# Retention and a feed-forward layer on one core: block 0's stores go ahead of the transposing transfers, and four other steps change places

## The chip, the core and the metric

The kernel runs on one core of a Trainium2 chip. The core has a matrix engine (TensorE, in the rows PE, its weight loads PEld), VectorE (DVE), ScalarE (ACT), GpSimd (POOL) and SyncE (SP). Only PE multiplies matrices; it writes to PSUM, eight banks of 128 partitions by 2 KB. DVE and ACT read PSUM, POOL reads and writes only SBUF, the working memory. Transfers between memory and SBUF are issued here by SP (nearly all), by POOL (the weights) and by ACT (a few), and 16 DMA engines carry them out. The metric is the device time of one execution in microseconds, the median of several runs.

## The reference

For every batch b of 4 and head h of 8, over 768 positions t, with 64 values per head:

```
state = gamma[h] * state + outer(k[t], v[t])      # 64 x 64
y[t]  = (1/8) * q[t] @ state
```

Then x is y with the heads side by side, 3072 tokens of 512 values, and

```
hid = x @ w_in                                    # 512 -> 2048
g   = max(hid, 0) + alpha * min(hid, 0)           # alpha per hidden column
out = g @ w_out                                   # 2048 -> 512, float32
```

## The kernel before

**Tiles and blocks.** The 3072 tokens are cut into twelve units of 256 tokens (a unit is u in the code, three to a batch; the change's short name calls them tiles), and two units make a block n, of six. Retention is done by chunks of 128 tokens (c = 0, 1 of a unit), with a running 64 x 64 state for each head.

**Retention of a unit.** `load` (line 132) brings k, q and v. `rescale` (L152) multiplies k and q by powers of gamma into the fp16 tile kdq; `cast_v` (L166 on ACT, L168 on POOL) makes vx, v in fp16. kq, which holds k and q with the head's values along the partitions, comes from kdq either by PE (`turn_pe`, L182, units 0 to 3) or by a transposing transfer on SP's queue (`turn_dma`, L172, units 4 to 11). `sum_mm` (L215) forms a chunk's sum of outer products; `state` adds it to the running state on DVE (L239, tile ss), multiplies by the decay (L240 on POOL, tile tf; at a batch's first chunk L236 on DVE does that alone) and copies it to fp16 tiles tg (L251 on ACT, L253 on POOL). `score_mm` (L265, tiles sca and scb) forms k q products, `masks` (L277, tiles m) applies the causal mask on DVE, and `out_mm` (L294 with tg, L309 with m) gives y, which ACT copies into xT (L327).

**Feed-forward of a block.** `ffn1(n)` is 64 matmuls of 512 columns (L374) in sixteen turns of four: a turn fills one PSUM bank hps, ACT takes from it hm = relu(-hps) (L385, three buffers), and DVE makes gt (L387) from both. In block 1 the first eight of the sixteen hidden column groups are split by unit: eight turns of eight matmuls with 256 columns, then eight of four with 512. Block 0's second product is `ffn2`, 64 matmuls in four tiles of 128 tokens (ops, L410); ACT copies each tile into os (L419), SP stores it (L423). os has three buffers, so the fourth copy waits for the first store to land.

Blocks 1 to 5 use `ffn2_seven`: the product of 2 x 2 quarters in seven quarter products instead of eight, each of 16 matmuls of 256 columns (L453, banks ox, oy, oz). It needs sums of quarters: of the weights once (`w_sums`, L345, tile wsum) and of the tokens in each block (`g_sums`, L358, tile gs, four sums i = 0 to 3 over eight column groups, which can be cut by lo and hi). Between products ACT keeps a partial result (L468, tile cu) and DVE adds another to it (L473).

**What sets the order.** The order is written by hand: each engine carries out its instructions in the order of the program, and waits where an operand or a buffer isn't ready. `ffn1`, `ffn2` and `ffn2_seven` are generators; `tick(gen, m)` lets one go on by m matmuls, and the retention steps of the next block stand between the ticks. A quarter product takes 16 ticks. `gen` is `ffn2(0)` ahead of the loop and `half` is `ffn1(1)`. `behind(i, gate)` makes POOL's rescaling wait for a DVE sum.

Of the kernel before, what the change touches and what calls it, by code (L numbers as in the profile page):

```python
# [21 lines left out]
def kernel(  # L22
# [13 lines left out]
    NFT = d_ff // 128  # L36
# [45 lines left out]
    HF, HM = NFT // 2, d_model // 2  # L82
    wsum = sbp.tile([128, 4, HF, HM], F16, tag="wsum", name="wsum")

    def ps(bank, name, dt=FP, n=512):
        return psp.tile([128, n], dt, tag=f"b{bank}", name=name)
# [34 lines left out]
    def load(u, parts="kqv"):  # L121
        b, c = divmod(u, UPB)
        t = staged.setdefault(u, {})
        for nm in parts:
            src = {"k": k, "q": q, "v": v}[nm[0]]
            if nm[0] not in t:
                t[nm[0]] = sbp.tile(
                    [128, H, 2 * D], FP, tag=f"{nm[0]}s", bufs=3, name=f"{nm[0]}s{u}"
                )
            h = slice(0, H) if len(nm) == 1 else slice(4 * int(nm[1]), 4 * int(nm[1]) + 4)  # L130
            hold(
                nc.sync.dma_start(  # L132
                    out=t[nm[0]][:, h, :],
                    in_=src[b, h, U * c : U * c + U, :].rearrange(
                        "h (p r) d -> p h (r d)", r=2
                    ),
                )
            )
# [23 lines left out]
    def cast_v(eng, u, h0=0, h1=H):  # L162
        o = unit(u)[2][:, h0:h1].rearrange("p h r d -> p (h r d)")
        i = staged[u]["v"][:, h0:h1].rearrange("p h x -> p (h x)")
        if eng is nc.scalar:
            eng.activation(out=o, in_=i, func=COPY, bias=0.0, scale=1.0)  # L166
        else:
            eng.tensor_copy(out=o, in_=i)  # L168

    def turn_dma(u):  # L170
        kdq, kq, _ = unit(u)
        nc.sync.dma_start_transpose(out=kq, in_=kdq.rearrange("p t r h d -> p (t r h d)"))  # L172
# [54 lines left out]
    def state(u, c, eng, copy="gg"):  # L227

        if (u, c) in sums:
            state_copy(state_sum(u, c, eng), copy)  # L230
# [43 lines left out]
    def masks(u, hh, parts=(0, 1)):  # L274
        for a in parts:
            m2 = sbp.tile([128, 2, 2, 128], F16, tag=f"m2{a}{hh}", bufs=2, name=f"m2{a}{hh}")
            nc.vector.tensor_tensor(  # L277
                out=m2,
                in0=live[u, hh][a].rearrange("p (r a i) -> p r a i", r=2, a=2),
                in1=mask.unsqueeze(2).to_broadcast([128, 2, 2, 128]),  # L280
                op=MULT,
            )
            live[u, hh][a] = m2
# [53 lines left out]
    def w_sums(i, lo, hi):  # L337

        w = w_out_all.rearrange("p (k f) (j e) -> p k f j e", k=2, j=2)
        w12, w21, w22 = w[:, 0, lo:hi, 1, :], w[:, 1, lo:hi, 0, :], w[:, 1, lo:hi, 1, :]  # L340
        t1, t2, t3, t4 = (wsum[:, x, lo:hi, :] for x in range(4))
        o, a, b = (
            (t1, w12, w[:, 0, lo:hi, 0, :]), (t2, w22, t1), (t3, w22, w12), (t4, w21, t2)
        )[i]
        return nc.vector.tensor_tensor(out=o, in0=a, in1=b, op=SUB)  # L345

    def g_sums(n, i, lo, hi):

        if n not in gsums:
            gsums[n] = sbp.tile([128, 4, HF, U], F16, tag="gt", bufs=2, name=f"gs{n}")  # L350
        g = gts[n].rearrange("p (k f) (j t) -> p k f j t", k=2, j=2)
        a11, a12 = g[:, 0, lo:hi, 0, :], g[:, 1, lo:hi, 0, :]
        a21, a22 = g[:, 0, lo:hi, 1, :], g[:, 1, lo:hi, 1, :]
        s1, s2, s3, s4 = (gsums[n][:, x, lo:hi, :] for x in range(4))
        o, a, b, op = (
            (s1, a21, a22, ADD), (s2, s1, a11, SUB), (s3, a11, a21, SUB), (s4, a12, s2, SUB)
        )[i]
        return nc.vector.tensor_tensor(out=o, in0=a, in1=b, op=op)  # L358

    def ffn1(n, banks, apart=0):  # L360


        gt = sbp.tile([128, NFT, TB], F16, tag="gt", bufs=2, name=f"gt{n}")
        gts[n] = gt
        turns = [(f, 2, ul, ul + 1) for ul in range(2) for f in range(0, apart, 2)]
        rest = range(apart, NFT)
        if apart == 0:
            rest = [f + x for f in range(HF) for x in (0, HF)]
        turns += [(f, 1, 0, 2) for f in rest]
        for i, (f0, nf, lo, hi) in enumerate(turns):  # L370
            hps = ps(banks[i % len(banks)], "hps").rearrange("p (f t) -> p f t", f=nf)
            for f in range(nf):
                for hp in range(4):
                    nc.tensor.matmul(  # L374
                        out=hps[:, f, :].rearrange("p (u t) -> p u t", t=U),
                        lhsT=w_in_all[:, hp, 128 * (f0 + f) : 128 * (f0 + f) + 128],
                        rhs=xT[n][:, lo:hi, hp, :],
                        start=(hp == 0),
                        stop=(hp == 3),
                    )  # L380
                    if f < nf - 1 or hp < 3:
                        yield
            hm = sbp.tile([128, TB], FP, tag="hm", bufs=3, name="hm")
            hm = hm.rearrange("p (f t) -> p f t", f=nf)
            nc.scalar.activation(out=hm, in_=hps, func=RELU, bias=0.0, scale=-1.0)  # L385
            for f in range(nf):
                nc.vector.scalar_tensor_tensor(  # L387
                    out=gt[:, f0 + f, U * lo : U * hi],
                    in0=hm[:, f, :],
                    scalar=oma_sb[:, f0 + f : f0 + f + 1],  # L390
                    in1=hps[:, f, :],
                    op0=MULT,
                    op1=ADD,
                )
            if n > 0 and f0 in (HF + 5, NFT - 1):
                lo, hi = (0, 6) if f0 < NFT - 1 else (6, HF)
                g_sums(n, 0, lo, hi)
                g_sums(n, 1, lo, hi)
            yield
# [136 lines left out]
    def tick(gen, m=10**6):  # L536
        for _ in range(m):
            if next(gen, 1) == 1:
                return
# [13 lines left out]
    V, G, A = nc.vector, nc.gpsimd, nc.scalar  # L553
# [84 lines left out]
    get_wo(2)  # L638
    out_mm(1, (4, 5))
    gen = ffn1(0, (2, 3, 6, 7, 0, 1, 2, 3, 6, 7, 4, 5, 0, 1, 2, 3), apart=4)  # L640
    tick(gen)


    gen = ffn2(0, (0, 1, 2, 3), parts=4)
    half = ffn1(1, (6, 7, 4, 5, 4, 5, 0, 1, 2, 3, 0, 1, 4, 5, 6, 7), apart=8)
    turn_pe(2, 0, 5)
    tick(gen, 5)
# [12 lines left out]
    rescale(G, 3, 0, 4, 8)  # L660
    rescale(G, 3, 1, 4, 8)
    cast_v(G, 3)
    tick(gen, 9)
    out_mm(2, (4, 5))
    tick(gen, 10)
# [6 lines left out]
    masks(3, 0)  # L672
    sum_mm(3, (6, 7))
    state(3, 0, G, "ga")
    w_sums(0, 0, HF)
    for i in range(1, 4):
        w_sums(i, 0, 4)
    tick(gen, 8)
# [4 lines left out]
        gate = w_sums(i, 4, HF)  # L683
    behind(rescale(G, 4, 0, 0, 8), gate)
    rescale(G, 4, 1, 0, 8)
    cast_v(A, 4)
    turn_dma(4)
    load(6)
    rescale(G, 5, 0, 0, 8)
    rescale(G, 5, 1, 0, 8)  # L690
    tick(gen, 8)
    out_mm(3, (6, 7))
    tick(gen)
    turn_dma(5)
    load(7)
    tick(half, 8)
    cast_v(A, 5)
    tick(half)
# [2 lines left out]
    for n in range(1, NBLK):  # L701
        more = n + 1 < NBLK
        u0 = 2 * (n + 1)
        if n > 1:
            gen = ffn1(n, (7, 2, 3, 1, 0, 6, 5, 4, 7, 1, 0, 4, 5, 6, 7, 1))
            if more:
                for u in (u0, u0 + 1):
                    i = rescale(G, u, 0, 0, 8)
                    if u == u0:
                        behind(i, gate)  # L710
                    rescale(G, u, 1, 0, 8)
                    turn_dma(u)
                    cast_v(G, u)
                    if u + 2 < NU:
                        load(u + 2)
                    tick(gen, 8)
            tick(gen)
        gen = ffn2_seven(n, 0, 1, None if more else 2)
        if more:
            tick(gen, 8)  # L720
            sum_mm(u0, (2, 3))
            sum_mm(u0 + 1, (2, 3), half=1)
            score_mm(u0, 0, (4, 5))
            score_mm(u0, 1, (6, 7))
            state(u0, 0, G)
            masks(u0, 0)
            masks(u0, 1)
            tick(gen, 25)
            state(u0, 1, G)
            state(u0 + 1, 0, G)  # L730
            state(u0 + 1, 1, G)
            g_sums(n, 2, 0, HF)
            tick(gen, 16)
            out_mm(u0, (4, 5))
            score_mm(u0 + 1, 0, (6, 7))
            score_mm(u0 + 1, 1, (2, 3))
            masks(u0 + 1, 0)
            masks(u0 + 1, 1)
            gate = g_sums(n, 3, 0, HF)
            tick(gen, 32)  # L740
            out_mm(u0 + 1, (4, 5))
        else:
            g_sums(n, 2, 0, HF)
            g_sums(n, 3, 0, HF)
        tick(gen)
# [30 lines left out]
```

## Time and profile before

| | |
|---|---|
| median of 3 runs | 234.12 us (233.09 to 235.04) |
| profiled execution | 232.69 us |
| its span, first to last instruction | 231.0 us |
| PE busy | 199.8 us, 86% |
| DVE busy | 157.1 us, 68% |
| ACT busy | 100.2 us, 43% |
| POOL busy | 86.5 us, 37% |
| chain that ended last | PE 63%, DVE 17%, DMA 6%, ACT 4%, POOL 4% |
| mean granted TensorE clock | 0.97 |

The profile is of one execution. The busy shares are means over the whole span: PE is the engine with the most work, yet 31 us of the span pass without any on it, and where these lie is read from the timeline and the waits, not from the shares.

### The profile page before, as it was taken

Reading aid. Unit: us, or ns where it says so; the run is one execution under the profiler, and the core shown is the slowest. Engines: PE = TensorE matmul, PEld = TensorE weight load, DVE = VectorE, ACT = ScalarE, POOL = GpSimd, SP = SyncE. Lnnn points to the kernel's source line nnn. Section 1 sums busy time; section 2 is a strip of 40 time slices with the busy share of each in tenths; the row PEclk is TensorE's granted clock in tenths of the full one; section 3 lists DMA queues with packets and bytes.
Section 4 is the critical chain, followed back from the end, with each engine's and each line's share of the span. In section 5 each row is a group of like instructions: output and inputs, shape, how many; then the busy total and the mean of one; then the engine's idle time right before and its main releaser. Section 6 shows DMA issues by size and latency. Waiting matters only on the chain.

```text
span 231.0 us, 5497 instructions
## 1 busy us (share of the span) xinstructions
PE 199.8 (86%) x2314; PEld 128.8 (56%) x2314; DVE 157.1 (68%) x247; ACT 100.2 (43%) x162; POOL 86.5 (37%) x102
## 2 busy tenths in 40 slices
PE   7789999987803789899988899989899898999892
PEld 2457445753600348774467764478744587644781
DVE  6885874369002798828996648999278986389930
ACT  2376762544104532356623346613466333466121
POOL 2486085633940004694016692025960062000000
PEclk9999999999965699999999999999999999999998
DMA  6999997999099911039971159941290010300013
GB/s 173 340 189 154 214 288 121 268 334 301 2 271 297 287 57 47 3 128 266 251 223 50 45 144 285 246 150 48 93 210 19 3 48 31 108 0 0 0 48 136
DMA packets 64840, 33.94 MB, mean 147 GB/s; under 512 B 18080, under 2 KB 64304, under 8 KB 64816
## 3 DMA queue, kind: packets, MB, share of 16 engines
q1 hardware_dynamic: 60272, 29.30, 44.7%
q0 software_dynamic: 4224, 4.19, 11.4%
q8 instruction: 18, 0.29, 0.6%
q10 hardware_dynamic: 320, 0.10, 0.2%
q14 instruction: 6, 0.05, 0.1%
HBM read 27.30 MB, written 6.29 MB: 145 GB/s over the span
## 4 chain that ended last, share of the span: by engine, by line
PE 63%; DVE 17%; DMA 6%; ACT 4%; POOL 4%; SPq 3%; issue 2%; DVEq 0%; POOLq 0%; ACTq 0%
PE hps L374 28%; PE ox L453 13%; PE oy L453 10%; DVE gt L387 6%; DVE gs L358 4%; PE ops L410 3%; DMA out_dram<-os 3%; SPq L132 2%; DMA ks<-in_k_dram 2%; PE y L309 2%; DVE wsum L345 2%; ACT hm L385 2%; DVE m L277 2%; PE y L294 2%; POOL kdq L152 2%
## 5 line engine op out<-in xcount | busy, mean ns | idle before, releaser
L374 PE MATMUL hps<-xT,win 128*128 128x512 f16 (+1 forms) x432 | 87.0, 362 | 11.7 <-ACT os L419 10.0
L387 DVE SCALAR_TENSOR_TENSOR gt<-hm,oma,hps 128x512 f16<-128x512 f32 (+1 forms) x108 | 71.5, 685 | 35.1 <-ACT hm L385 28.5
L385 ACT ACTIVATE hm<-hps 128x512 f32<-128x512 f32 x96 | 57.1, 597 | 36.3 <-PE hps L374 32.3
L374 PEld LDWEIGHTS <-win 128*128 128x128 f16 x432 | 42.6, 99 | 53.8 <-issue 12.7
L240 POOL TENSOR_TENSOR tf<-ss,tab 128x256 f32<-128x256 f32 x16 | 10.5, 658 | 60.8 <-DVE ss L239 60.4
L453 PEld LDWEIGHTS <-gs 128*128 128x128 f16 x320 | 31.0, 98 | 3.9
L453 PEld LDWEIGHTS <-gt 128*128 128x128 f16 x240 | 22.7, 98 | 10.9 <-DVE gt L387 6.0
L468 ACT ACTIVATE cu<-ox 128x512 f32<-128x512 f32 x15 | 9.0, 597 | 44.0 <-PE ox L453 44.0
L253 POOL CAST tg<-tf 64x256 f16<-64x256 f32 x35 | 19.3, 550 | 17.9 <-DVE tf L236 16.2
L152 POOL TENSOR_TENSOR kdq<-ks,tab 128x1024 f16<-128x1024 f32 (+1 forms) x12 | 19.4, 1614 | 15.6 <-DMA ks<-in_k_dram 9.6
L473 DVE TENSOR_TENSOR os<-oy,cu 128x512 f32<-128x512 f32 x14 | 9.7, 690 | 19.4 <-PE oy L453 16.3
L327 ACT ACTIVATE xT<-y 128x512 f16<-128x512 f32 x24 | 16.2, 740 | 11.1 <-PE y L309 11.1
L152 POOL TENSOR_TENSOR kdq<-qs,tab 128x1024 f16<-128x1024 f32 (+1 forms) x13 | 20.4, 1572 | 1.0 <-DMA qs<-in_q_dram 0.9
L453 PE MATMUL ox<-wsum,gs 128*128 128x256 f16 x160 | 19.1, 273 | 0.0
L277 DVE TENSOR_TENSOR m<-sca,mi 128x512 f16<-128x512 f32 x24 | 16.4, 683 | 2.3 <-PE scb L265 2.3
L277 DVE TENSOR_TENSOR m<-scb,mi 128x512 f16<-128x512 f32 x24 | 16.3, 679 | 0.0
L453 PE MATMUL ox<-wout,gt 128*128 128x256 f16 x80 | 11.6, 274 | 4.2 <-DVE gt L387 4.1
L410 PE MATMUL ops<-wout,gt 128*128 128x512 f16 x64 | 15.2, 380 | 0.0
L168 POOL CAST vx<-vs 128x1024 f16<-128x1024 f32 (+1 forms) x11 | 10.5, 962 | 8.4 <-DMA vs<-in_v_dram 8.4
L358 DVE TENSOR_TENSOR gs<-gt 128x1536 f16<-128x1536 f16 (+2 forms) x15 | 13.0, 868 | 0.3
L453 PE MATMUL ox<-wsum,gt 128*128 128x256 f16 x80 | 10.4, 273 | 3.2 <-ACT cu L468 2.7
L239 DVE TENSOR_TENSOR ss<-tf,st 128x256 f32<-128x256 f32 x16 | 6.6, 415 | 5.9 <-POOL tf L240 3.6
(51 smaller groups left out, 170.8 us busy)
## 6 DMA issues: line engine op xcount, KB each, us to landing
out_dram<-os SPq DMA_DIRECT2D x23, 256.0 KB, 2.3
vs<-in_v_dram SPq DMA_DIRECT2D x10, 512.0 KB, 6.4
ks<-in_k_dram SPq DMA_DIRECT2D x8, 512.0 KB, 4.4
qs<-in_q_dram SPq DMA_DIRECT2D x8, 512.0 KB, 5.3
ks<-in_k_dram SPq DMA_DIRECT2D x8, 256.0 KB, 5.1
qs<-in_q_dram SPq DMA_DIRECT2D x8, 256.0 KB, 5.4
win<-in_moe_w_in_dram POOLq DMA_DIRECT2D x4, 512.0 KB, 7.2
wout<-in_moe_w_out_dram POOLq DMA_DIRECT2D x4, 512.0 KB, 7.9
```

The source lines that it names most:

```text
L152: return eng.tensor_tensor(out=kdq[:, t, :, h0:h1, :].rearrange("p r h d -> p h r d"), in0=staged[u]["kq"[t]][:, h0:h1, :].rearrange("p h ...
L168: eng.tensor_copy(out=o, in_=i)
L240: eng.tensor_tensor(out=t, in0=ss, in1=dec, op=MULT)
L253: nc.gpsimd.tensor_copy(out=o, in_=i)
L277: nc.vector.tensor_tensor(out=m2, in0=live[u, hh][a].rearrange("p (r a i) -> p r a i", r=2, a=2), in1=mask.unsqueeze(2).to_broadcast([128, ...
L327: nc.scalar.activation(out=xT[n][:, ul, :, 128 * c : 128 * c + 128].rearrange("k a (p r) -> k a r p", r=2), in_=ys[c].rearrange("k (a r p) ...
L358: return nc.vector.tensor_tensor(out=o, in0=a, in1=b, op=op)
L374: nc.tensor.matmul(out=hps[:, f, :].rearrange("p (u t) -> p u t", t=U), lhsT=w_in_all[:, hp, 128 * (f0 + f) : 128 * (f0 + f) + 128], rhs=x ...
L385: nc.scalar.activation(out=hm, in_=hps, func=RELU, bias=0.0, scale=-1.0)
L387: nc.vector.scalar_tensor_tensor(out=gt[:, f0 + f, U * lo : U * hi], in0=hm[:, f, :], scalar=oma_sb[:, f0 + f : f0 + f + 1], in1=hps[:, f, :],
L410: nc.tensor.matmul(out=opss[tq], lhsT=gt[:, ft, 128 * tq : 128 * tq + 128], rhs=w_out_all[:, ft, :], start=(ft == 0), stop=(ft == NFT - 1),)
L453: nc.tensor.matmul(out=o[:, m, :], lhsT=lhs(f, m), rhs=rhs(f), start=(first and m == 0 and f == 0), stop=(f == HF - 1), skip_group_check=True,
```

## The change

The changed kernel does the same work in another order. Five edits:

1. Ahead of the loop, the transposing transfers of units 4 and 5 and the loads of units 6 and 7 are issued after the last tick of `ffn2(0)`, and so behind its four stores on SP's queue; ACT's casts of v for units 4 and 5 stand behind the first and the second activation of `ffn1(1)`'s second half.
2. `w_sums(0)`, the first of the four weight sums, stands behind unit 2's masks on DVE instead of behind unit 3's first masks and state.
3. In `ffn1(n)` the first two token sums are cut at four column groups instead of six, and the first cut comes after the turn with f0 = 11 instead of 13: in blocks 2 to 5 after eight turns of sixteen instead of twelve, in block 1 four turns from the end instead of two.
4. In the loop, the state add of chunk 1 of the first unit stands between its two pairs of masks. The ticks ahead of `out_mm` are 8, 25 and 15 instead of 8, 25 and 16, so both visits of `out_mm` come when a quarter product is complete.
5. In block 5 the third and fourth token sum stand behind 33 ticks.

```diff
@@ ffn1
-            if n > 0 and f0 in (HF + 5, NFT - 1):
-                lo, hi = (0, 6) if f0 < NFT - 1 else (6, HF)
+            if n > 0 and f0 in (HF + 3, NFT - 1):
+                lo, hi = (0, 4) if f0 < NFT - 1 else (4, HF)
                 g_sums(n, 0, lo, hi)
                 g_sums(n, 1, lo, hi)
@@ ahead of the loop
     rescale(G, 3, 1, 4, 8)
     cast_v(G, 3)
+    w_sums(0, 0, HF)
     tick(gen, 9)
...
     sum_mm(3, (6, 7))
     state(3, 0, G, "ga")
-    w_sums(0, 0, HF)
     for i in range(1, 4):
         w_sums(i, 0, 4)
...
     rescale(G, 4, 1, 0, 8)
-    cast_v(A, 4)
-    turn_dma(4)
-    load(6)
     rescale(G, 5, 0, 0, 8)
     rescale(G, 5, 1, 0, 8)
     tick(gen, 8)
     out_mm(3, (6, 7))
     tick(gen)
+    turn_dma(4)
+    load(6)
     turn_dma(5)
     load(7)
+    tick(half, 8)
+    cast_v(A, 4)
     tick(half, 8)
     cast_v(A, 5)
     tick(half)
@@ the loop
             state(u0, 0, G)
             masks(u0, 0)
+            state(u0, 1, G)
             masks(u0, 1)
             tick(gen, 25)
-            state(u0, 1, G)
             state(u0 + 1, 0, G)
             state(u0 + 1, 1, G)
             g_sums(n, 2, 0, HF)
-            tick(gen, 16)
+            tick(gen, 15)
             out_mm(u0, (4, 5))
...
         else:
+            tick(gen, 33)
             g_sums(n, 2, 0, HF)
             g_sums(n, 3, 0, HF)
```

SP's queue ahead of the loop. L132 loads a unit's k, q or v, L172 transposes, L423 stores a tile of block 0. Before:

```order
L132 DMA vs_457<-in_v_dram 128x8x128
L172 DMA_TRANSPOSE kq_1021<-kdq_1020 128x16x128
L132 DMA ks_1027<-in_k_dram 128x8x128
L132 DMA qs_1029<-in_q_dram 128x8x128
L132 DMA vs_1031<-in_v_dram 128x8x128
L423 DMA out_dram<-os 128x512 x4
L172 DMA_TRANSPOSE kq_1034<-kdq_1033 128x16x128
```

and now:

```order
L132 DMA vs_457<-in_v_dram 128x8x128
L423 DMA out_dram<-os 128x512 x4
L172 DMA_TRANSPOSE kq_1021<-kdq_1020 128x16x128
L132 DMA ks_1098<-in_k_dram 128x8x128
L132 DMA qs_1100<-in_q_dram 128x8x128
L132 DMA vs_1102<-in_v_dram 128x8x128
L172 DMA_TRANSPOSE kq_1026<-kdq_1025 128x16x128
```

The four stores stood behind unit 4's transposing transfer (kq_1021) and unit 6's load; now they stand behind unit 5's load (vs_457) alone.

DVE in block 2, from the end of `ffn1(2)` on: gt are the activations, gs the token sums, tf and ss the states, m the masks. Before:

```order
L387 SCALAR_TENSOR_TENSOR gt_1627<-hm,oma,hps 128x512 x12
L358 TENSOR_TENSOR gs_1737<-gt_1627 128x1536
L358 TENSOR_TENSOR gs_1737<-gs_1737,gt_1627 128x1536
L387 SCALAR_TENSOR_TENSOR gt_1627<-hm,oma,hps 128x512 x4
L358 TENSOR_TENSOR gs_1737<-gt_1627 128x512
L358 TENSOR_TENSOR gs_1737<-gs_1737,gt_1627 128x512
L236 TENSOR_TENSOR tf_0_1885<-st_1783,tab 128x256
L277 TENSOR_TENSOR m_1889<-sca,mi 128x512
L277 TENSOR_TENSOR m_1891<-scb,mi 128x512
L277 TENSOR_TENSOR m_1893<-sca,mi 128x512
L277 TENSOR_TENSOR m_1895<-scb,mi 128x512
L473 TENSOR_TENSOR os<-oy,cu 128x512
```

and now:

```order
L387 SCALAR_TENSOR_TENSOR gt_1627<-hm,oma,hps 128x512 x8
L358 TENSOR_TENSOR gs_1705<-gt_1627 128x1024
L358 TENSOR_TENSOR gs_1705<-gs_1705,gt_1627 128x1024
L387 SCALAR_TENSOR_TENSOR gt_1627<-hm,oma,hps 128x512 x8
L358 TENSOR_TENSOR gs_1705<-gt_1627 128x1024
L358 TENSOR_TENSOR gs_1705<-gs_1705,gt_1627 128x1024
L236 TENSOR_TENSOR tf_0_1885<-st_1783,tab 128x256
L277 TENSOR_TENSOR m_1889<-sca,mi 128x512
L277 TENSOR_TENSOR m_1891<-scb,mi 128x512
L239 TENSOR_TENSOR ss_1_1894<-tf_0_1885,st_1784 128x256
L277 TENSOR_TENSOR m_1899<-sca,mi 128x512
L277 TENSOR_TENSOR m_1901<-scb,mi 128x512
```

The two large sums moved from four turns before the end to eight and got shorter, the last two got longer, and the state add ss of chunk 1 moved ahead of the second pair of masks.

PE in block 2, the second visit of `out_mm` (unit 7, tiles y). Before:

```order
L453 MATMUL ox<-wsum,gs_1737 128x256
L453 LDWEIGHTS gt_1627
L453 MATMUL ox<-wsum,gt_1627 128x256
L294 LDWEIGHTS tg_73
L294 MATMUL y_2089<-kq_1645,tg_73 128x128
```

and now:

```order
L453 LDWEIGHTS gs_1705
L453 MATMUL ox<-wsum,gs_1705 128x256
L294 LDWEIGHTS tg_73
L294 MATMUL y_2088<-kq_1645,tg_73 128x128
L294 LDWEIGHTS tg_73
```

The first matmul of the sixth product, which writes to bank ox that ACT has yet to copy, stood ahead of the visit; now the visit follows the fifth product's last matmul.

## Rows read from the trace of the kernel before

**Rows 1.** Page, part 2: granted clock in tenths, forty slices of 5.8 us.

```profile
PEclk9999999999965699999999999999999999999998
```

**Rows 2.** Chain of waits, stretch 55 to 82 us: start, length, engine and line.

```profile
62.37 1.71 SPq L172
...
66.53 5.56 DMA out_dram<-os
...
72.19 0.60 ACT os L419
72.78 0.49 ACT hm L385
73.27 0.94 ACT vx L166
...
74.74 1.66 DVE gt L387 x4
```

**Rows 3.** Timeline of PE, 44 to 102 us: start, length, operation, idle before in brackets.

```profile
55.96 0.38 PE L294 MATMUL y<-kq,tg 128*128 128x128 f16 x4 [1.42 <-DVE ss L239]
...
58.36 4.52 PE L374 MATMUL hps<-xT,win 128*128 128x256 f16 x36
72.84 1.86 PE L374 MATMUL hps<-xT,win 128*128 128x512 f16 x4 [9.95 <-ACT os L419]
...
86.31 0.21 PE L265 MATMUL scb<-kq 64*64 64x128 f16 x1 [0.45 <-DVE gt L387]
```

**Rows 4.** By stage: window, length, busy PE PEld DVE ACT POOL, clock, DMA share, GB/s.

```profile
57.00:58.00 1.00, 1.00 (x6) 0.45 (x5) 1.00 (x2) 1.00 (x2) 0.96 (x2) 1.00 0.30 91
...
65.00:66.00 1.00, 0.00 (x0) 0.00 (x0) 0.00 (x0) 0.00 (x0) 1.00 (x1) 0.90 0.96 182
66.00:72.00 6.00, 0.00 (x0) 0.00 (x0) 0.00 (x0) 0.00 (x0) 0.06 (x1) 0.50 1.07 339
```

**Rows 5.** Who PE waited for, 100 to 135 us (block 2): total, times, longest.

```profile
PE scb L265 <- DVE ss L239: 1.1, 1, 1.1
PE ox L453 <- DVE gt L387: 1.0, 1, 1.0
PE ox L453 <- ACT cu L468: 0.7, 1, 0.7
```

**Rows 6.** Timeline of SP, whole span, its DMA queue.

```profile
52.10 1.40 SPq L132 DMA_DIRECT2D vs<-in_v_dram  x1
...
107.81 4.63 SPq L172 DMA_TRANSPOSE kq<-kdq  x1
```

**Rows 7.** View of transfers: engine, count, KB each, median us from issue to landing.

```profile
out_dram<-os SPq DMA_DIRECT2D x23, 256.0 KB, 2.3
...
kq<-kdq SPq DMA_TRANSPOSE x8, 3.9
```

**Rows 8.** Timeline of DVE, 44 to 102 us.

```profile
44.25 2.62 DVE L387 SCALAR_TENSOR_TENSOR gt<-hm,oma,hps 128x256 f16<-128x256 f32 x6 [5.14 <-ACT hm L385]
...
53.00 0.68 DVE L345 TENSOR_TENSOR wsum<-wout 128x1024 f16<-128x1024 f16 x1
...
56.34 1.09 DVE L345 TENSOR_TENSOR wsum<-wout 128x1024 f16<-128x1024 f16 x1
```

**Rows 9.** Timeline of DVE, 100 to 231 us (block 2).

```profile
113.53 0.96 DVE L358 TENSOR_TENSOR gs<-gt 128x1536 f16<-128x1536 f16 x1
...
115.40 2.72 DVE L387 SCALAR_TENSOR_TENSOR gt<-hm,oma,hps 128x512 f16<-128x512 f32 x4
```

**Rows 10.** Table by stage, end of block 2, columns as in rows 4.

```profile
101.60:115.40 13.80, 13.80 (x67) 6.26 (x65) 11.49 (x15) 8.96 (x15) 4.71 (x4) 1.00 0.96 247
115.40:117.60 2.20, 1.16 (x9) 0.64 (x7) 2.20 (x5) 0.60 (x1) 0.00 (x0) 1.00 1.14 340
```

**Rows 11.** Timeline of POOL, 44 to 102 us.

```profile
56.95 1.55 POOL L253 CAST tg<-tf 64x256 f16<-64x256 f32 x2
...
64.16 1.90 POOL L152 TENSOR_TENSOR kdq<-qs,tab 128x1024 f16<-128x1024 f32 x1
```

## What the change will do to the time

> **What bounds the kernel now.** Read the granted clock by slices first [rows 1]: it is full but for the 12th to the 14th slice (63.5 to 80.9 us). Then the timeline of PE around them [rows 3]: PE stands still for 9.95 us, from 62.9 to 72.84, until ACT has copied an os tile. The table by stage shows the clock fall to half only after PE had stopped (mean 0.90 in 65 to 66, then 0.50 [rows 4]); it came back late in the 14th slice, some 3 us after PE had gone on at 76.45. The chain of waits tells why PE stopped [rows 2]. SP's queue is served in order. Its transposing transfer of unit 4 had to wait for POOL, went out at 62.37, three loads followed, and only then the first of block 0's stores, which landed 5.56 us after its issue at 66.53. ACT's fourth copy (72.19) needs that store's buffer, and the activations of `ffn1(1)` stand behind the copy on ACT; PE needs their banks. So one store's place in a queue holds three engines.
>
> In the blocks behind it PE is the bound, with short waits. In block 2 there are three [rows 5]: 1.0 us for the last-but-one activation gt, 1.1 us for a state add, 0.7 us for ACT's copy cu. The views of blocks 3 and 4 show the 1.0 and the 0.7 again, block 5 the 1.0, block 1 the 0.7.
>
> The profiled execution took 232.69 us, 1.7 more than its span of 231.0 and 1.4 less than the median of 234.12. I sum against the profiled one.
>
> **Edit 1, the queue.** The first store will be issued when SP has done with unit 5's load, 52.10 + 1.40 = 53.5 [rows 6], and its tile is copied by then. It queues behind that load, whose traffic ends at about 57.3 (DMA share 0.30 in 57 to 58 [rows 4]). A store of 256 KB at the 339 GB/s that the engines moved in 66 to 72 [rows 4] takes 0.8 us, so it lands at about T = 58.1. Without any queueing it would be 53.9 + 2.3 = 56.2 [rows 7], with the worst landing, 5.56, it would be 59.5. I take 58.1, since the store of rows 2 too landed only when the load ahead of it had.
>
> From T on ACT runs in order: copy 0.59, hm 0.49, cast 0.95, hm 0.5, cast 0.95, hm 0.5 (0.59, 0.49 and 0.95 are differences of starts in [rows 2], with the second cast priced as the first), 3.98 in all; that is the third turn of `ffn1(1)`'s second half. DVE then has two turns of two gt at 1.66 / 4 = 0.415 [rows 2], 1.66; four turns at 2.72 / 4 = 0.68 [rows 9], 2.72; two token sums of 1024 columns, which I price as the weight sum of that width, 0.68 [rows 8], 1.36; and four turns, 2.72. Sum 8.46. The last gt of block 1 is ready at 58.1 + 3.98 + 8.46 = 70.5. PE is not the later one: its twelve turns of this half start at 58.36 less the wait of edit 2, 56.9; the first five take 4.5 us [rows 3], the other seven 0.86 each (edit 3), and it stops about 1 us at the seventh for a bank that DVE has yet to empty: some 68.5. Before, PE got that last gt at 86.3 [rows 3]. **Gain 15.7 us**; with T at 59.5 it is 14.3, with T at 56.2 PE's own first turn decides (hm at 57.8 instead of 58.7), and it is 16.6.
>
> What is late next: the transposing transfers, moved past the stores. Unit 4's still waits for POOL alone (62 us, all stores issued by then) and PE wants kq only at 69.7, over 3 us after a landing of 3.9 [rows 7]. Unit 5's stands behind unit 6's load; such a one held SP 4.63 us [rows 6]. POOL is done with unit 5's kdq at about 65, SP with unit 6's load then too, so kq is there by 65 + 4.6 + 3.9 = 73.5; PE wants it at about 77. The loads of units 6 and 7 are needed by POOL at about 81 and 86, and go out by 72. The two casts on ACT end at 61.7, PE uses them at 69. All hidden, with 3 us and more to spare.
>
> **Edit 2, w_sums(0).** 1.22 us leave DVE's queue at 51, where they were ahead of unit 3's masks, and with them PE's wait of 1.42 [rows 3]. They go where DVE sat idle 5.14 us ahead of 44.25 [rows 8]; nothing there is queued behind them. The gain at 56 is counted in edit 1 and nearly lost again in waiting for the store: 0 by itself.
>
> **Edit 3, the cut of the token sums.** Before, the two sums of 1536 columns hold DVE from 113.53 to 115.40 [rows 9], 1.87 us, four turns before the end. A turn is 13.8 / 16 = 0.86 us for PE [rows 10] and 0.68 for DVE, so DVE wins back 0.18 a turn, and gt of the eighth column group is still 1 us late. Now 1.36 us are lost after the eighth turn and 7 x 0.18 = 1.26 won back by the fifteenth: 0.1 late. Four blocks (2 to 5) x about 1.1 (the 1.0 of [rows 5] and the matmuls just ahead of it that are late too): **4.4 us**. Bounds: 0, if DVE falls behind elsewhere, and 5.2 (1.3 a block, as 7 matmuls with that wait end 1.3 later than without).
>
> **Edit 4, order in the loop.** The visit at the fifth product's end gives PE 36 or 40 matmuls while ACT copies ox: the 0.7 goes in blocks 1 to 4, **2.8 us** (0 to 3.4, as the empty stretch with its pipeline is 0.85). It needs the second unit's masks earlier; counting DVE's queue through the block in the timeline's durations, I find them done about 0.4 us ahead of PE, the thinnest margin here. The earlier state add lets POOL multiply under two masks; the 1.1 of block 2 goes, **1.0 us** (0 to 1.1).
>
> **Edit 5.** DVE frees bank oy ahead of two sums instead of behind them. PE would now come 1 us earlier and wait about 0.5 for it; so nothing is lost: 0.
>
> Sum: 15.7 + 4.4 + 2.8 + 1.0 = 23.9. Span 207.1, profiled time 208.8; taking a little for the median I predict **209 us**. The term bounds give 14.3 to 16.6 for edit 1 and 0 to 9.7 for the rest; half of the rest lost is 213.
>
> **A rule against the change.** The weight sum that took 0.68 alone took 1.09 beside POOL's copies [rows 8, 11]. So DVE's sums of two SBUF tiles and POOL's work slow each other, and edit 3 moves two such sums nearer to POOL's rescaling. In block 2 POOL has 4.71 us of work from 101.6 on [rows 10], and the sums would come at 110, 3.7 us behind its end. In block 1 POOL's last rescaling, 1.90 us, ends at 66.1 before [rows 11], now at about 65; the sums come at 66.6.
> The Trainium skill (SBUF — State Buffer, Who interferes with whom) says that a DVE instruction with two SBUF inputs and a GpSimd one that reads SBUF exclude each other, and the later one waits for the whole of the other. By that rule a late rescaling would cost its full 1.9 us in block 1, where the row's 0.4 would be the measured price.
>
> **Rivals.**
> A. *The store lands late, or the clock still falls.* For: the loads do stand ahead of the store, and PE still pauses, 1 us at turn 11 (2.4 with T at 59.5). Against: the 1.42 us wait of [rows 3] left the clock full. Price: 1.4 for the store; if the clock is at half for 3 us of work, as it was after PE went on at 76.45, some 1.5 to 3.5 more. 210 to 214. Chance 0.15.
> B. *DVE becomes the bound in the loop.* For: in 115.4 to 117.6 it was busy 2.20 of 2.20 [rows 10]; the sums' total stays. Against: in 101.6 to 115.4 it was busy 11.49 of 13.8, room for the 1.36. Edits 3 and 4 lose half to all of 8.2: 213 to 217. Chance 0.15.
> C. *Sums and rescaling meet* in block 1, by the mechanism above: 0.4 to 1.9 us, 209.2 to 211. Chance 0.06.
> D. *Slower.* The clock, once fallen, stays at 1.2 GHz. A block's `ffn1` then takes 27.6 instead of 13.8 us [rows 10], its seven products as much more, so that from about 48 us at half clock on, two thirds of two blocks, the 24 us are lost: 234 and above. Against it: in this trace the clock came back once PE had work again, and then stayed full to the end [rows 1]. Chance 0.01.
> E. *The change doesn't do what it says*: the stores still wait, for a reason that the chain hides, and only the loop gains: 232.7 - 8.2 = 224.5. Against: the load ahead was over by 57.3 [rows 4], and ACT waited on to 72. Chance 0.03.
>
> My forecast, 206.5 to 211, has 0.60. The range 206 to 214 takes in A, C and the near half of B; what is left out is E, D and the far half of B. A measurement here tells about 1% from no change: faster by more 0.97, within 0.01, slower 0.02.
>
> **What would show it.** Edit 1: the first L423 store issued near 54, landed by 59, no PE wait for os, clock full in all slices up to the end, the last gt of block 1 near 70.5. Edit 3: no PE wait of 1.0 for gt in blocks 2 to 5. Edit 4: no wait for cu at L453, none for ss in block 2. Wrong would make it: a PE wait for kq or vx at 70 to 77, a half clock slice past 60, or a wait of `out_mm` for masks in the place of that for cu.

## The result, and the profile after

The changed kernel takes 211.65 us, median of 4 runs (209.73 to 213.89), against 234.58 for the kernel before (233.09 to 236.17, 4 runs). The ratio is 0.895, 95% interval 0.885 to 0.906: faster; it leaves out two of the four executions, 212.94 and 213.89 us, whose mean granted clock was lower (0.991 and 0.989, against 0.998 and 0.999 in the other two). The profiled execution took 210.36 us, its span is 208.6 (predicted: 208.8 and 207.1), so of the 23.9 us that the sum promised 22.4 came.

**Block 1.** The page of the kernel after, part 2, busy tenths of PE and granted clock in forty slices of 5.2 us; it answers to [rows 1]:

```profile
PE   7799999997995999999999999999999999999991
...
PEclk9999999999999999999999999999999999999999
```

The three slices at half clock are gone. What is left of the stall is the 5 in PE's thirteenth slice. The chain of waits of the kernel after, 55 to 75 us (start, length, engine and line), answers to [rows 2]:

```profile
54.98 5.59 DMA out_dram<-os
...
60.68 0.60 ACT os L419
61.28 0.49 ACT hm L385
...
61.79 0.95 ACT vx L166
...
63.33 0.94 ACT vx L166
...
64.80 4.30 DVE gt L387 x8
...
69.12 0.70 DVE gs L358
...
70.54 2.64 DVE gt L387 x4
...
73.22 0.21 PE scb L265
```

It runs as the prediction wrote it down: store, copy, activation, cast, activation, cast, activation, eight gt, two sums, four gt. But it starts late: the first store landed at 60.6 instead of 58.1. SP's timeline shows part of it (start, length, operation), beside [rows 6]:

```profile
52.95 1.40 SPq L132 DMA_DIRECT2D vs<-in_v_dram  x1
54.98 6.65 SPq L423 DMA_DIRECT2D out_dram<-os  x4
61.93 1.41 SPq L172 DMA_TRANSPOSE kq<-kdq  x1
...
66.27 4.77 SPq L172 DMA_TRANSPOSE kq<-kdq  x1
```

Unit 5's load left SP at 54.35, 0.85 later than before. The store left at 54.98, as soon as ACT had copied its tile (54.36 to 54.96), and landed 5.6 us after its issue, 1.0 more than the estimate gave it. The load ahead of it, unit 5's v, is in the view of transfers issued from 50 to 64 us, before and now (KB, us from issue to landing):

```profile
vs<-in_v_dram SPq DMA_DIRECT2D x1, 512.0 KB, 6.4
```

```profile
vs<-in_v_dram SPq DMA_DIRECT2D x1, 512.0 KB, 7.0
```

This load landed at 52.10 + 6.4 = 58.5 before and at 52.95 + 7.0 = 59.95 now, and the store 0.6 us behind it. Behind the stores the transposing transfers came as foreseen, the second with its 4.77 us on SP; no matmul waited for kq or vx in block 1's second product. PE's timeline (idle before in brackets) answers to [rows 3]:

```profile
57.94 5.38 PE L374 MATMUL hps<-xT,win 128*128 128x256 f16 x40
65.72 5.35 PE L374 MATMUL hps<-xT,win 128*128 128x512 f16 x24 [2.40 <-ACT hm L385]
```

The pause ahead of the seventh turn is 2.40 us, not 9.95, and the clock stayed full through it. The last gt was ready at 73.2 (row 73.22 of the chain), before it was at 86.3.

**The loop.** PE's waits of the kernel after in block 2, 86 to 120 us (total, times, longest), in the place of the three of [rows 5]:

```profile
PE scb L265 <- DVE ss L239: 0.6, 1, 0.6
```

The waits for gt and cu are gone, the one for the state add fell from 1.1 to 0.6. In blocks 3 and 4 no wait is left. DVE's timeline in block 2 answers to [rows 9]: the first two sums hold it for 1.33 us (96.15 to 97.48) after eight gt, and eight more gt follow without a gap.

```profile
89.32 6.79 DVE L387 SCALAR_TENSOR_TENSOR gt<-hm,oma,hps 128x512 f16<-128x512 f32 x8 [0.80 <-ACT hm L385]
96.15 0.69 DVE L358 TENSOR_TENSOR gs<-gt 128x1024 f16<-128x1024 f16 x1
...
97.48 5.54 DVE L387 SCALAR_TENSOR_TENSOR gt<-hm,oma,hps 128x512 f16<-128x512 f32 x8
```

PE's timeline gives each block's start, the first matmul of `ffn1(n)`; the differences tell blocks apart, and the experiments below are read by them. For block 2 the rows are, before and now:

```profile
101.56 13.98 PE L374 MATMUL hps<-xT,win 128*128 128x512 f16 x64
```

```profile
87.63 13.98 PE L374 MATMUL hps<-xT,win 128*128 128x512 f16 x64
```

Starts, lengths and spans of the profiles compared (us; "end" is from the start of `ffn1(5)` to the end of the span):

| kernel | ffn1(2) starts | block 2 | block 3 | block 4 | end | span |
|---|---|---|---|---|---|---|
| before | 101.56 | 33.23 | 31.93 | 32.14 | 32.14 | 231.0 |
| after | 87.63 | 30.56 | 29.72 | 29.95 | 30.74 | 208.6 |
| e1 queue alone | 87.33 | 33.24 | 31.92 | 32.15 | 32.06 | 216.7 |
| e2 fourth buffer | 87.30 | 33.24 | 31.93 | 32.14 | 32.09 | 216.7 |
| e4 loop alone | 100.80 | 30.56 | 29.72 | 29.94 | 30.78 | 221.8 |
| f1 old cut | 87.50 | 31.20 | 31.08 | 31.30 | 32.12 | 213.2 |
| f2 old visits | 88.87 | 31.30 | 30.58 | 31.07 | 30.78 | 212.6 |
| f3 old state add | 88.38 | 31.82 | 29.72 | 30.24 | 30.74 | 210.9 |
| f4 old weight sum | 86.33 | 30.57 | 29.72 | 29.95 | 30.73 | 207.3 |
| h0 casts back | 89.08 | 30.56 | 29.73 | 29.95 | 30.78 | 210.1 |
| h1 buffer, casts back | 84.54 | 30.55 | 29.73 | 29.95 | 30.73 | 205.5 |
| h2 buffer, late casts | 85.10 | 30.57 | 29.73 | 29.95 | 30.75 | 206.1 |

Of the 22.4 us, 13.9 came before `ffn1(2)`, 2.7, 2.2 and 2.2 in blocks 2 to 4, and 1.4 in block 5.

### The profile page after: what moved, and what is told of

It is laid out like the page before. It is cut to its first block, busy times and chain, and to the rows that moved or that the text cites. A ratio compares the mean times of both kernels' runs of the same rounds, so it can differ in the third digit from the quotient of the medians.

```text
span 208.6 us, 5498 instructions
## 1 busy us (share of the span) xinstructions
PE 196.0 (94%) x2314; PEld 128.6 (62%) x2314; DVE 155.3 (74%) x247; ACT 100.5 (48%) x162; POOL 85.5 (41%) x102
## 4 chain that ended last, share of the span: by engine, by line
PE 74%; DMA 9%; DVE 8%; ACT 3%; POOL 3%; issue 1%; DVEq 0%; POOLq 0%; ACTq 0%
PE hps L374 33%; PE ox L453 15%; PE oy L453 12%; DMA vs<-in_v_dram 5%; DMA out_dram<-os 4%; DVE gt L387 3%; PE kps L91 3%; PE ops L410 2%; PE y L309 2%; PE sca L265 2%; PE y L294 2%; DVE m L277 2%; PE st L215 1%; DVE ss L239 1%; POOL vx L168 1%; POOL tf L240 1%
## 5 line engine op out<-in xcount | busy, mean ns | idle before, releaser
L374 PE MATMUL hps<-xT,win 128*128 128x512 f16 (+1 forms) x432 | 84.5, 355 | 2.4 <-ACT hm L385 2.4
L387 DVE SCALAR_TENSOR_TENSOR gt<-hm,oma,hps 128x512 f16<-128x512 f32 (+1 forms) x108 | 70.2, 685 | 20.7 <-ACT hm L385 15.8
L374 PEld LDWEIGHTS <-win 128*128 128x128 f16 x432 | 42.1, 98 | 42.6 <-DVE gt L387 3.1
L240 POOL TENSOR_TENSOR tf<-ss,tab 128x256 f32<-128x256 f32 x16 | 12.2, 760 | 42.3 <-DVE ss L239 40.6
L253 POOL CAST tg<-tf 64x256 f16<-64x256 f32 x35 | 16.8, 479 | 16.6 <-DVE tf L236 14.9
L358 DVE TENSOR_TENSOR gs<-gt 128x1024 f16<-128x1024 f16 (+1 forms) x15 | 13.0, 868 | 0.3
L188 ACT ACTIVATE kq<-trb 128x1024 f16<-128x1024 f16 x8 | 8.2, 1022 | 6.4 <-PE trb L182 6.3
L453 PE MATMUL ox<-wout,gt 128*128 128x256 f16 x80 | 10.4, 274 | 0.0
L91 PE MATMUL kps<-spin 128*128 128x512 f16 x25 | 8.5, 480 | 1.9 <-DVE spin L558 1.5
```

What stands on the lines that cost most here:

```text
L91: nc.tensor.matmul(out=pt, lhsT=spin[:, 0:128], rhs=spin, start=True, stop=True)
L240: eng.tensor_tensor(out=t, in0=ss, in1=dec, op=MULT)
L253: nc.gpsimd.tensor_copy(out=o, in_=i)
L374: nc.tensor.matmul(out=hps[:, f, :].rearrange("p (u t) -> p u t", t=U), lhsT=w_in_all[:, hp, 128 * (f0 + f) : 128 * (f0 + f) + 128], rhs=x ...
L387: nc.vector.scalar_tensor_tensor(out=gt[:, f0 + f, U * lo : U * hi], in0=hm[:, f, :], scalar=oma_sb[:, f0 + f : f0 + f + 1], in1=hps[:, f, :],
L453: nc.tensor.matmul(out=o[:, m, :], lhsT=lhs(f, m), rhs=rhs(f), start=(first and m == 0 and f == 0), stop=(f == HF - 1), skip_group_check=True,
```

## Experiments

The theory: the place of block 0's stores in SP's queue held ACT through the os buffer, and PE through ACT; in the loop, three waits went. Its rivals: something else in edit 1 (the casts, the traffic, the half clock), and a loop gain that only follows from the earlier part.

**e1, the queue alone.** The kernel before with

```
     cast_v(A, 4)
-    turn_dma(4)
-    load(6)
...
     tick(gen)
+    turn_dma(4)
+    load(6)
     turn_dma(5)
     load(7)
```

> The kernel before with one step of the change: the transposing transfers and loads of units 4 to 7 are issued behind block 0's four stores; the casts of v on ACT and all else stay. If the stores' place in SP's queue is the cause of the stall, as the prediction says, the stall of 9.95 us at the L419 copy shrinks to under 3 us, the clock stays full, and the last gt of block 1 comes at 72 to 74 us instead of 86.3: span 217 to 219, time 219 to 221, ratio about 0.94. Rival: the moved casts of v on ACT carry a good part of it; then the gain here is under 9 us, time above 224.

Measured: 218.62 us, ratio 0.935 (0.925 to 0.944), span 216.7. PE's timeline shows the second half of `ffn1(1)` and nothing between its matmuls:

```profile
58.48 10.56 PE L374 MATMUL hps<-xT,win 128*128 128x256 f16 x64
```

The stall is gone entirely, 14.2 us by the start of `ffn1(2)`. The rival is out: the gain needs no moved cast. Block 1 stalls even less than in the kernel after, whose start of `ffn1(2)` is no earlier although edits 3 and 4 work for it.

**e2, a buffer.** The kernel before, with its queue, and

```
-  os_sb = sbp.tile([128, d_model], FP, tag="os", bufs=3, name="os")
+  os_sb = sbp.tile(
+      [128, d_model], FP, tag="cu" if tq == 3 else "os", bufs=3, name="os"
+  )
```

> The kernel before with SP's queue as it was, but the fourth copy of block 0's output tiles goes into a buffer that is free (one of tile cu's), so that it does not wait for the first store to land. If the wait for the buffer is what holds ACT and with it PE, the stall goes although the stores still leave at 66.5: last gt of block 1 near 71, span about 215.5, time about 217, ratio 0.93. Rival: the queue itself holds more than the buffer (the loads or kq come too late, or the transfers' traffic slows the activations); then a stall of several us stays at another instruction and the time is above 222.

Measured: 218.7 us, ratio 0.932 (0.925 to 0.939), span 216.7, as e1. SP's timeline has the transposing transfer still at 62.45 and the stores still at 66.6, behind three loads:

```profile
62.45 1.70 SPq L172 DMA_TRANSPOSE kq<-kdq  x1
...
66.61 4.39 SPq L425 DMA_DIRECT2D out_dram<-os  x4
```

but ACT's copies (two in one row, 58.20) and its activations don't wait:

```profile
58.20 1.10 ACT L421 ACTIVATE os<-ops 128x512 f32<-128x512 f32 x2
59.58 0.60 ACT L385 ACTIVATE hm<-hps 128x512 f32<-128x512 f32 x1 [0.28 <-PE hps L374]
```

So the queue did harm through one buffer alone: the same 14 us come from moving the store or from not needing it. The span is 1.2 above my 215.5, since `ffn1(1)` is now paced by PE and the sums' old cut.

**e3 and e3b, the price of the half clock.** The kernel before with matmuls on a constant tile in the stall (`keep`, 45), and then with 48 there and 13 in the next pause:

```
     tick(half, 8)
     cast_v(A, 5)
+    tick(half, 28)
+    keep(48, 7)      # e3: keep(45, 7)
+    tick(half, 4)    # e3b alone
+    keep(13, 7)      # e3b alone
     tick(half)
```

> The kernel before, with 45 matmuls of 512 columns on a constant tile put on PE where it stalls (they write to a bank that nothing reads then). The stall stays, PE is busy in it, and the clock should stay full. This prices the half clock by itself. By the table by stage of before, VectorE and ScalarE bound most of the stretch behind the stall, so I expect 1.5 to 3 us: time 229.5 to 231.5, ratio 0.985 to 0.995. Rival: the half clock is the main loss, 13.65 us at half, so 5 to 7 us: time 225.5 to 227.5, ratio 0.97.

Measured for e3: 235.7 us, ratio 1.008 (1.004 to 1.013): no gain, and if anything a little slower, for which no run shows a reason. PE's timeline and the table by stage (window, length, busy PE, PEld, DVE, ACT, POOL, clock, DMA share, GB/s):

```profile
62.48 9.88 PE L91 MATMUL kps<-spin 128*128 128x512 f16 x45
73.80 1.02 PE L374 MATMUL hps<-xT,win 128*128 128x512 f16 x4 [1.45 <-ACT os L419]
77.42 6.71 PE L374 MATMUL hps<-xT,win 128*128 128x512 f16 x24 [2.59 <-DVE gt L387]
```

```profile
62.00:72.00 10.00, 10.00 (x48) 4.50 (x47) 0.00 (x0) 0.00 (x0) 3.81 (x3) 1.00 0.90 261
...
76.00:77.00 1.00, 0.00 (x0) 0.00 (x0) 1.00 (x4) 0.95 (x3) 0.00 (x0) 0.90 1.27 290
77.00:78.00 1.00, 0.58 (x2) 0.28 (x3) 1.00 (x3) 0.81 (x2) 0.00 (x0) 0.50 0.79 176
```

The clock stayed full through the stall and fell at 76.8, in the pause behind PE's next turn; since the last of the 45 matmuls, at 72.4, PE had worked 1.0 us. It was back at 80.2, so the half clock lasted 3.4 us instead of 13.65. From the os copy (73.15) to the last gt (87.12) it still took 13.97 us, before 14.07. So some 10 us fewer at half clock were worth nothing, because PE had nothing to do in most of them; but turns behind the stall were still at half, and the run didn't price those. Hence e3b:

> The kernel before with matmuls on a constant tile in both pauses of PE in block 1: 48 in the stall for the os copy and 13 in the next one, which waits for a bank. In the first kernel of this kind the clock fell later, in that second pause, and no time was gained. Here it should stay full. VectorE then waits no more for turns that PE makes at half clock: by the timeline of before (idle 0.56, 0.68 and the like ahead of three gt) the last gt comes 14.1 - 1.7 = 12.4 us behind the os copy, so 1 to 2 us are gained: time 232 to 233.2, ratio 0.99 to 0.997. Rival: the half clock costs nothing at all, since VectorE is the bound there: ratio 1.00.

Measured for e3b: 233.05 us, ratio 0.994 (0.990 to 0.997), clock full all through block 1. Its PE, and its DVE with twelve gt in one piece:

```profile
64.07 10.52 PE L91 MATMUL kps<-spin 128*128 128x512 f16 x48
...
76.31 2.97 PE L91 MATMUL kps<-spin 128*128 128x512 f16 x13
79.11 5.34 PE L374 MATMUL hps<-xT,win 128*128 128x512 f16 x24
```

```profile
77.35 6.79 DVE L387 SCALAR_TENSOR_TENSOR gt<-hm,oma,hps 128x256 f16<-128x256 f32 x12 [0.56 <-ACT hm L385]
...
86.05 1.40 DVE L387 SCALAR_TENSOR_TENSOR gt<-hm,oma,hps 128x512 f16<-128x512 f32 x2
```

Its os copy, and the last gt of the kernel before:

```profile
74.80 0.60 ACT L419 ACTIVATE os<-ops 128x512 f32<-128x512 f32 x1 [14.72 <-DMA out_dram<-os]
```

```profile
84.86 1.40 DVE L387 SCALAR_TENSOR_TENSOR gt<-hm,oma,hps 128x512 f16<-128x512 f32 x2
```

The os copy came at 74.80 and the last gt at 87.45, 12.65 us later; in the kernel before it was 72.19 [rows 2] and 86.26, 14.07. The half clock cost 1.4 us of the 14 that went with the stall (e1, e2).

The Trainium skill (TensorE: Matmul & The Clock Gate, Terms) prices throttled time at its length times the clock's missing share. With rows of this case that gives an estimate of 13.65 us x 0.5 = 6.8 us; the measurement is 1.4 and decides: for most of that time PE was waiting, and then DVE was busy nearly without a gap.

**e4, the loop alone.** The kernel before with edits 3, 4 and 5 (their lines of the diff).

> The kernel before with edits 3, 4 and 5 alone (cut of the token sums, state add between the masks, visits at the products' ends, block 5's sums later); the queue ahead of the loop, the casts and the first weight sum stay. If the loop's gain is its own, the span falls by 8 to 9.5 us and the stall stays: span 221.5 to 223, time 223 to 225, ratio 0.96. Rival: the loop's gain depends on the earlier part (loads that are earlier, no half clock); then it is under 5 us here, ratio above 0.98.

Measured: 224.2 us, ratio 0.957 (0.948 to 0.967), span 221.8. The blocks' periods are those of the kernel after to 0.04 us: the loop's gain is its own, 9.2 us, and it adds to e1's, nearly: by the spans the two separate gains make 23.5, together they gave 22.4.

**f1 to f4, one edit undone in the kernel after.** f1 has edit 3's cut at six again, f2 `tick(gen, 16)`, f3 the state add behind both pairs of masks, f4 `w_sums(0, 0, HF)` behind unit 3's state.

> The changed kernel with edit 3 undone: the first token sums are cut at six column groups and come after f0 = 13, as before. If the sums' place holds the last-but-one gt back, a wait of 1.0 us for gt comes back in each of blocks 2 to 5, and block 1's last gt is up to 1 us later: span 212.5 to 214 against 208.6, ratio to the kernel before about 0.915. Rival: DVE has the same work either way and the time only moves to another wait; span within 1 us of 208.6.

Measured for f1: 215.82 us, ratio 0.920 (0.913 to 0.927). The four waits are back, in one row of PE's waits (total, times, longest):

```profile
PE ox L453 <- DVE gt L387: 4.1, 4, 1.0
```

By the table it costs 0.64, 1.36, 1.35 and 1.38 us in blocks 2 to 5, 4.7 in all (4.4 predicted). In block 2 part of it only fills the wait for the state add. In block 1 the last gt came 13.4 us behind the fourth os copy (59.65 to 73.05) instead of 12.5 (60.68 to 73.17): 0.9 more, which the span hides because the store landed 1.0 us earlier in this execution.

> The changed kernel with the visits of out_mm where they were, one matmul into the fourth and the sixth quarter product (16 ticks for 15). If the visit hides ACT's copy cu, the wait of 0.7 us comes back in blocks 1 to 4: span 211 to 211.7 against 208.6, ratio about 0.906. Rival: without it the second visit comes later and finds its masks ready, which now are the tight operand; then it costs under 1 us.

Measured for f2: 214.82 us, ratio 0.917 (0.913 to 0.922), span 212.6. The wait for cu is back four times:

```profile
PE ox L453 <- ACT cu L468: 2.7, 4, 0.7
```

The table gives 1.24 ahead of block 2 (block 1's last gt was ready at 73.19, as in the kernel after, so this is the visits' doing), then 0.74, 0.86 and 1.12: 4.0 us, more than the 2.8 of the idle time alone and above my bound of 3.4. Ahead of block 2 and in block 4 it is more than the wait; that the visit starts later also by the matmul ahead of it, and that DVE's next block feels it, is argued and not shown.

> The changed kernel with the state add of chunk 1 behind both pairs of masks again. If its place under the masks is what shortened block 2's wait for a state add (1.06 before, 0.58 after the change), the wait is about 1.1 again and block 2's period 31.0 to 31.1 instead of 30.56; blocks 3 and 4 stay within 0.1 of 29.72 and 29.95. Rival: the shorter wait came from the sums' new cut, which lets DVE end earlier; then block 2 stays within 0.1 of 30.56.

Measured for f3, in one execution: 212.64 us, span 210.9. Block 2 takes 31.82, more than the 31.1 expected, and block 4 30.24, so the edit is worth 1.3 and 0.3 us, 1.6 in all, against 1.0 predicted; in block 4 no row had shown a wait. Its PE waits, and its clock around the pause in block 1:

```profile
PE hps L374 <- ACT hm L385: 2.4, 1, 2.4
PE scb L265 <- DVE ss L239: 1.4, 1, 1.4
```

```profile
63.00:64.00 1.00, 0.00 (x0) 0.00 (x0) 0.57 (x2) 1.00 (x3) 1.00 (x2) 1.00 1.27 289
...
67.00:68.00 1.00, 1.00 (x4) 0.30 (x2) 0.76 (x2) 0.53 (x1) 0.00 (x0) 0.50 1.15 348
...
70.00:71.00 1.00, 1.00 (x6) 0.48 (x5) 0.96 (x2) 0.59 (x1) 0.00 (x0) 1.00 1.14 238
```

The pause of 2.4 us for an activation is that of the kernel after, but here the clock fell 1.3 us after PE had gone on at 65.06, was at half in 67 to 68, and was back by 70. So the pause that is left can bring the half clock or not: the rival A of the prediction, seen once. The last gt came 13.5 us behind the copy instead of 12.5: 1 us.

> The changed kernel with edit 2 undone: the first weight sum stands on DVE behind unit 3's first masks and state again. The prediction priced edit 2 at nothing: the wait of about 1.4 us ahead of unit 3's out_mm comes back, but the first store's landing decides what follows, so span 208 to 209.2. Rival: the moved sum, beside POOL's issue of the last weight transfer, delays the weights and the loads behind them and so the first store (it landed at 60.6, not at 58.1); then undoing it makes the first store land near 58 to 59 and the span 206 to 207.5.

Measured for f4: 209.39 us, ratio 0.896 (0.889 to 0.902), span 207.3. The wait ahead of unit 3's `out_mm` is back, the pause in block 1 is shorter:

```profile
PE y L294 <- DVE ss L239: 1.5, 1, 1.5
...
PE hps L374 <- ACT hm L385: 0.5, 1, 0.5
```

The first store landed at 59.3 instead of 60.6, and the span lies in the range that the rival gave. So edit 2 shows no gain. Whether it costs anything, as the rival says, stays open: with it the first store landed at 60.6, 59.6, 60.6 and 59.9 (after, f1, f2, f3), without it at 59.0 and 59.3 (e1, f4); but unit 5's load, which it lands behind, left SP at 53.6 to 54.9 us in seven profiles with the edit and at 53.3 to 54.8 in seven without, and these overlap. In h0, which has edit 2, unit 3's came so late that PE waited for them:

```profile
PE trb L182 <- POOL kdq L152: 2.5, 3, 1.6
```

**h0 to h2, what was left.** h0 puts the casts back, h1 that and e2's buffer, h2 the buffer with the casts later still:

```
h0, h1:
     rescale(G, 4, 1, 0, 8)
+    cast_v(A, 4)
...
     tick(half, 8)
-    cast_v(A, 4)
-    tick(half, 8)
     cast_v(A, 5)
h2:
-    tick(half, 8)
+    tick(half, 32)
     cast_v(A, 4)
```

> The changed kernel with ACT's two casts of v where they were: unit 4's ahead of the first os copy, unit 5's behind the first activation of the second half. Block 1's last gt came at 73.2 with both casts between the activations; one cast less behind the store's landing should save about 0.95 us of ACT's queue: last gt 71.6 to 72.4, ffn1(2) starts at 86 to 87 instead of 87.6, span 207 to 208. Rival: the cast ahead of the copies makes the first store leave later by as much (its wait for v ends at 53.5 to 54.5), and nothing is gained: span 208.3 to 209.

Measured for h0: 209.21 us, ratio 0.896 (0.890 to 0.902). Inconclusive: the interval lies within that of the kernel after, and the profiled execution, 211.79 us, is the one with the late loads. From `ffn1(1)`'s first activation of the second half (63.09) to the last gt (74.6) it took 11.5 us, against 12.0 (61.17 to 73.2) in the kernel after.

> The changed kernel with both: the casts where they were, and the fourth os copy in a free buffer, so that ACT doesn't wait for the first store at all. If the store's landing near 60 is all that still holds block 1, the activations start when PE has made the first turn (about 58), PE no longer waits in ffn1(1), and the last gt comes at 69.5 to 70.5: ffn1(2) starts at 84 to 85, span 205 to 206, time 207 to 208, ratio 0.885. Rival: the loads of unit 5 (its v lands near 59) hold the cast and what stands behind it: span 207 or more.

> The changed kernel with the fourth copy in a free buffer and the two casts of v later, behind the fourth and the sixth activation of the second half. No activation then waits for a load or a store; PE's matmuls set the pace: twelve turns from 57 to 57.9, last gt 69 to 70, ffn1(2) starts at 83.5 to 84.7, span 204.5 to 205.7, time 206.5 to 207.5, ratio 0.88. Rival: the casts delay activations all the same, with the three hm buffers full, and it is no better than the kernel with the casts back.

Measured: h1 207.48 us, ratio 0.887 (0.882 to 0.891), span 205.5; h2 207.77 us, ratio 0.888 (0.884 to 0.893), span 206.1. ACT's copies in h1 come back to back, and the waits of PE from 44 us on show none in `ffn1(1)`:

```profile
57.23 1.09 ACT L421 ACTIVATE os<-ops 128x512 f32<-128x512 f32 x2
58.60 0.60 ACT L385 ACTIVATE hm<-hps 128x512 f32<-128x512 f32 x1 [0.28 <-PE hps L374]
```

```profile
PE st L215 <- POOL vx L168: 0.9, 1, 0.9
PE scb L265 <- DVE ss L239: 0.6, 1, 0.6
```

`ffn1(2)` starts at 84.54, 3.1 us earlier than in the kernel after. Of this 0.5 is an earlier start of `ffn1(1)`'s second half (57.47 for 57.94); some 2.6 the store's landing and the casts behind it still cost there. h1 is the fastest of all profiles here; in the ratios to the kernel before its interval overlaps that of the kernel after (0.885 to 0.906), so by the times it is not shown to be faster. Later casts are no better: in h2 the last activation waited 1.13 us for gt with its three buffers full.

## Why the prediction was right

**Edit 1.** Right in mechanism, 2.6 us too high: 15.7 at the last gt was predicted, 13.1 measured. The step that was mis-sized is T, the first store's landing: 60.6 for 58.1, beyond the 59.5 that I gave as the upper bound. The reason that I gave, that the store lands only behind the load ahead of it, holds: in every profile but h0 it landed 0.6 to 0.8 us behind that load's landing (in h0 it left SP only at 58.1 and took 2.7). But I took the load to be over at 57.3, where the engines' busy share ended, and it landed at 58.5, which the trace of before shows. That is about 1 us; the load came 0.85 later in the execution of the kernel after, and took 7.0 us instead of 6.4, 0.6 more. The store's tile was also not yet copied at 53.5, against what I had said: ACT ended that copy at 54.96, and the bound, which put the worst landing of rows 2 on an issue at 53.9, failed by that, since 54.98 + 5.56 is 60.5. All behind T was right to 0.2: 12.44 us predicted, 12.6 measured (60.57 to 73.18). The pause at the seventh turn was 2.4 instead of 1: T came 2.5 later and PE's first turn 1.0 (57.94 for 56.9).

The cover that I named held: no kq or vx was late in block 1's second product. The casts, hidden for their users, were not free for ACT: two of them stand between the store and the third activation. That I had counted in the chain, but not that a cast left ahead of the copies would have cost PE nothing, now that ACT hardly waits for the store (e1, h1).

**Edit 2** at nothing: no gain, right; that it costs nothing is not shown (f4). **Edit 3**: 4.4 predicted, 4.7 by f1. **Edit 4**: the visits 2.8 predicted, 4.0 by f2, since I priced the idle time and not what stands behind it; the state add 1.0 predicted, 1.6 by f3's one execution. Undone one by one the loop's edits are worth 10.3 us, together 9.2 (e4). By the table they add up in blocks 2, 3 and 5 (2.64, 2.22 and 1.42 us, together 2.67, 2.21 and 1.40); the difference lies in block 4 (2.76, together 2.19) and ahead of block 2 (1.24 in f2, 0.76 in e4), and its cause is open. The thin margin of the masks held: PE waited for no mask in the loop. **Edit 5** was not tried alone; PE's waits in block 5 show none for oy, and one of 0.5 us for ACT's last copies (os, L529).

**The rivals.** A came in its first half (the store late) and, in f3's execution, in its second; whether it did in other executions of the kernel after no trace shows. B did not come: from block 2 on no matmul waited for gt. C did not come: POOL's last rescaling ended at 65.6, block 1's sums started at 69.1 and took 0.69 each, as long as alone. D did not come: the clock was full in every slice, and in f3, where it fell, it was back after some 3.4 us. E did not come: the stores no longer stand behind the transposing transfer, and e1 and e2 show that this made the stall.

The time is 2.65 us above the forecast, 1.3%. The sum stands to the profiled execution as 208.8 to 210.36: the 2.6 too much at the last gt, less the 1.1 that the rest gave beyond its 8.2 (22.4 - 13.1 = 9.3). So the total is nearer than its largest term in part by luck, as two errors had opposite signs. The other 1.1 is the median, which lies 1.3 above the profiled execution where I had allowed 0.2.

## What to carry to other kernels

A store behind a waiting transfer in one queue holds its buffer, and through the buffer an engine that has nothing to do with either: look at what stands ahead of a store in its queue, and ask first whether one more buffer would make the question go away. Price a wait's removal by what ends next behind it, and take the landing of a transfer that queues from the landing of the one ahead of it (here 0.6 to 0.8 us behind that), not from its own issue (2.7 to 6.1 us after it in the kernels with the stores first) or from where the engines' busy share ends. Put a step that frees or fills a buffer where another engine would otherwise wait for a copy; its gain is the wait and the shift of all that follows.

## What the runs showed of the hardware

Half clock over 13.65 us (65.8 to 79.4, before) cost 1.4 us (e3b), as PE waited through 8.8 of them and DVE was busy beside most of the rest. Filling the stall with matmuls did not keep the clock: it fell 4.4 us behind the last of them, in the pause behind PE's next turn (e3). A pause of 2.4 us with the same work around it left the clock full in one execution (the kernel after) and was followed by half clock in another (f3). Unit 5's load left SP at 53.6 us in f3 and at 54.9 in f2, whose programs are the same up to there. A store of 256 KB that left SP well before the load ahead of it had landed took 3.9 us (e1) to 7.0 (e2), and landed 0.6 to 0.8 us behind the load, whatever its own issue.
